# Float64 weights split by bits: from an integer addition on GpSimd to shifts and merges on ScalarE and VectorE, with a scale of 256 left in the weights

## The chip, the core and the metric

The kernel runs on one core of a Trainium2 chip. The metric is the device time of one execution in microseconds. Three runs of the kernel before took 1601.95, 1603.39 and 1604.25 us; their median is 1603.39 us.

The core's engines are named as in the profile: PE (TensorE, the matrix unit; PEld is its weight load), DVE (VectorE), ACT (ScalarE), POOL (GpSimd) and SP (SyncE), which here issues all transfers.

## The reference

q, k and v have 8 batches of 8 heads of 576 tokens of 64 numbers, p has 32 packed queries for each batch and head, all in float32. With a softmax over the last axis, the reference computes

```python
p_packed = sm_attn(p, k, v)
x = sm_attn(q, p_packed, p_packed)
h = x @ w_in1
x = (h / (1 + exp(-h))) @ w_out1
h = x @ w_in2
out = (h * cos(h)) @ w_out2
```

x is laid out as 4608 tokens by 512. Both MLPs go from 512 to 2048 and back to 512. The four weight matrices come as float64, a type in which no engine of the kernel computes, so each weight has to be put together from its two 32-bit words. The low word is the first of the two. The high word holds the sign, 11 bits of exponent and the top 20 bits of the mantissa.

## The kernel before, in words

**Stages.** Tokens are worked on in blocks of 384 in the first MLP (three blocks for each pair of batches, four pairs) and of 512 in the second (nine blocks). Each block goes through the 16 chunks of 128 of the hidden size. So the first MLP has 192 steps (function first, line 850) and the second 144 (function second, line 925). Each step computes h for one chunk in PSUM, applies the activation, splits the result into a rounded part and a rest (split, line 518), and adds its product with w_out to the four accumulators acc. Each product is made of three matmuls (mm3, line 502), on the rounded part and the rest of both operands. For the first MLP w_in1 is multiplied by the packed values of each batch ahead of time (products, line 811), so that a step needs only the second softmax's result a and this product.

**The start.** Nothing of the first MLP can run before the first batch's attention and the first weights are done. At the start the first pair's 48 steps are cut into four groups of 12, one for each quarter of the hidden size. Each group needs four units of w_in1 (w1_unit, line 559) and four of w_out1 (wout1_unit, line 564). Meanwhile the second batch of the first pair goes through its attention. The weights of the second MLP are converted during the last pair (w2_unit, line 567), stored to memory as float32 pairs (w2dram), and loaded again when the second MLP begins.

**The conversion** is decode, lines 533 to 548. A unit is 128 partitions by 512 weights. There are 16 units of w_in1, 16 of w_out1 and 32 of the second MLP. For each unit, SP loads the words into a ring of tiles (wd; at the start also six tiles wde). Then

- ScalarE copies the absolute value of the high word, read as float32, to y (line 540);
- VectorE limits y to the range of the exponents that float32 can hold (a tensor_scalar, max and min), then shifts it left by 3 and masks it (a second tensor_scalar, on integers);
- ScalarE or VectorE, as the planner chooses, turns the low word into its top three bits, as an integer (lines 543 to 545);
- VectorE merges sign and top exponent bit of the high word with these three bits (a scalar_tensor_tensor on integers);
- GpSimd adds the two integers (line 547).

y is a tile named w or w1e for w_in1 and wy for the others. For wy, decode_parts (line 550) then copies the rounded part on ScalarE or VectorE and subtracts it on VectorE. w_in1's y goes to the matmuls of products and, through SP, to memory (w1dram).

**The order.** All instructions are first recorded in a Plan (line 79). Each has an engine, a price in ns (price, line 153) and the instructions that it must wait for. Some have two possible engines: a copy may go to ScalarE or VectorE, and the subtraction of split and two more element-wise steps may go to VectorE or GpSimd (combine, line 513). Due times of PE's steps follow from the list DUE (line 421) by interpolation, and those of all other instructions are worked back from them (order, line 358). A simulated run (schedule, line 277) then takes, on each free engine, the ready instruction that is due first; eight rounds are tried and the best is taken. The result is one fixed order for each engine's queue, SP's among them. In this simulated run, a VectorE instruction whose operands all lie in SBUF is charged extra when it begins while GpSimd is busy (lines 333 to 335).

All instructions are issued from one helper line, so every row of the trace has L194, and rows are told apart by their tiles.

Of the kernel before, what the change touches and what calls it, by code (L numbers as in the profile page):

```python
# [12 lines left out]
F32 = mybir.dt.float32  # L13
F32R = mybir.dt.float32r
I32 = mybir.dt.int32
U32 = mybir.dt.uint32
# [10 lines left out]

REBIAS = 896 << 20  # L30
WORD_MIN, WORD_MAX = (float(x) for x in np.array([REBIAS, REBIAS + 0x0FEFFFFF], np.int32).view(np.float32))


def f32(ap):
# [44 lines left out]
class Plan:  # L79
# [197 lines left out]
    def schedule(self, rank, reverse=False):  # L277


        ops = self.ops  # L280
        n = len(ops)
        if reverse:
            before, after = [o.after for o in ops], [o.before for o in ops]
        else:
            before, after = [o.before for o in ops], [o.after for o in ops]
        left = [len(a) for a in after]
        ready, start, taken = [0.0 if reverse else o.release for o in ops], [0.0] * n, [False] * n
        free = {e: 0.0 for e in (self.PE, self.DVE, self.ACT, self.POOL, self.DMA, self.NONE)}
        queue = {e: [] for e in free}
        coming = [(ready[i], i) for i in range(n) if not left[i]]  # L290
        heapq.heapify(coming)
        t = wire = 0.0
        done = 0

        def head(e):

            q = queue[e]
            while q and taken[q[0][1]]:
                heapq.heappop(q)
            return q[0][1] if q else None  # L300

        def take(e):

            q, aside = queue[e], []
            while (i := head(e)) is not None:
                heapq.heappop(q)
                o = ops[i]
                if reverse or not o.choice:
                    break
                end = t + o.choice[e][0] + (FAVOUR if e == self.DVE else -FAVOUR)  # L310
                if not any(f != e and head(f) == i and max(free[f], t) + o.choice[f][0] < end for f in o.choice):
                    break
                aside.append((rank[i], i))
            for x in aside:
                heapq.heappush(q, x)
            return i

        while done < n:
            while coming and coming[0][0] <= t:
                i = heapq.heappop(coming)[1]  # L320
                for e in (ops[i].engine,) if reverse else ops[i].choice or (ops[i].engine,):
                    heapq.heappush(queue[e], (rank[i], i))
            idle = True
            for e in queue:
                i = take(e) if free[e] <= t else None
                if i is None:
                    continue
                o = ops[i]
                if o.choice and not reverse:
                    o.engine, o.cost, o.emit = e, o.choice[e][0], [o.choice[e][1]]  # L330
                taken[i], start[i] = True, t
                end = t + o.cost
                if e == self.DVE and o.sbuf and not reverse and free[self.POOL] > t:
                    both = min(free[self.POOL] - t, o.cost / self.SHARED)
                    end += both * (1 - self.SHARED)
                free[e] = end
                if e == self.DMA:
                    if reverse:
                        wire = max(t, wire) + o.issue
                        end = wire + self.WIRE + o.cost  # L340
                    else:
                        end = wire = max(end + self.WIRE, wire) + o.issue
                        free[e] = max(free[e], wire - AHEAD)
                if reverse:
                    start[i] = end
                for j in before[i]:
                    lat = self.latency(ops[j], o) if reverse else self.latency(o, ops[j])
                    ready[j] = max(ready[j], end + lat)
                    left[j] -= 1
                    if not left[j]:  # L350
                        heapq.heappush(coming, (ready[j], j))
                done += 1
                idle = False
            if idle:
                t = min([free[e] for e in queue if free[e] > t and head(e) is not None] + [c[0] for c in coming[:1]])
        return start
# [30 lines left out]
def attention_mlps_kernel(  # L387
# [30 lines left out]
    SCALE = 1.0 / math.sqrt(D)  # L418
    plan = Plan(nc)

    DUE = [40e3, 205e3, 378e3, 550e3, 718e3]

    LATER = 380e3
    V, A, T, G, DMA = plan.V, plan.A, plan.T, plan.G, plan.D
# [108 lines left out]
    def decode(src, y):  # L533

        wd = rings["wd"]()
        flat = wd.rearrange("p f t -> p (f t)")
        DMA.dma_start(flat.rearrange("p (c f) -> p c f", c=src.shape[1]) if len(src.shape) == 3 else flat, src)
        lo, hi = wd[:, :, 0], wd[:, :, 1]
        y, yf = y.bitcast(I32), y.bitcast(F32)
        A.activation(yf, hi.bitcast(F32), AF.Abs)  # L540
        V.tensor_scalar(yf, yf, WORD_MIN, WORD_MAX, op0=ALU.max, op1=ALU.min)
        V.tensor_scalar(y, y, 3, 0x3FFFFFF8, op0=ALU.logical_shift_left, op1=ALU.bitwise_and)
        with plan.either():
            A.activation(lo, lo.bitcast(U32), AF.Copy, scale=2.0**-29)
            V.tensor_scalar(lo, lo.bitcast(U32), 2.0**-29, None, op0=ALU.mult)
        V.scalar_tensor_tensor(lo, hi, -(1 << 30), lo, op0=ALU.bitwise_and, op1=ALU.bitwise_or)
        G.tensor_tensor(y, y, lo, ALU.add)
        return flat

    def decode_parts(src, dst=None):  # L550
# [299 lines left out]
    def first(s):  # L850
# [15 lines left out]
        plan.due = None  # L866

        t = gfs()
        A.activation(t, h, AF.Tanh, scale=0.5)
        V.scalar_tensor_tensor(t, t, 1.0, h, op0=ALU.add, op1=ALU.mult)  # L870
        g = gs()
        split(g, t)
# [5 lines left out]
        if end:  # L878
            t0 = (pr * NA + blk) * TA
            dst = ypart[part - 1] if part else ydram  # L880
            for dm in range(KC):
                t = ysbs()
                with plan.either():
                    A.activation(t, acc[dm][:, :TA], AF.Copy, scale=0.5)
                    V.tensor_scalar(t, acc[dm][:, :TA], 0.5, None, op0=ALU.mult)
                DMA.dma_start(dst[dm, :, t0 : t0 + TA], t)


# [36 lines left out]
    def second(s):  # L925
# [8 lines left out]
            mm3(h, (w[:, 0, c], w[:, 1, c]), (y[:, 0], y[:, 1]), kc == 0, kc == KC - 1)  # L934
        plan.due = None
        n = nring()
        A.activation(n, h, AF.Copy, scale=INV_2PI, bias=ROUND)
        V.tensor_scalar(n, n, ROUND, None, op0=ALU.subtract)
        r = rring()
        V.scalar_tensor_tensor(r, n, -TWO_PI_HI, h, op0=ALU.mult, op1=ALU.add)  # L940
        V.scalar_tensor_tensor(r, n, -TWO_PI_LO, r, op0=ALU.mult, op1=ALU.add)
        V.tensor_scalar(r, r, 4.0, -4.0, op0=ALU.min, op1=ALU.max)
        A.activation(r, r, AF.Abs)
        A.activation(r, r, AF.Sin, scale=-1.0, bias=half_pi)
        V.tensor_tensor(r, r, h, ALU.mult)
        g = g2ring()
        split(g, r)
# [1 line left out]
        for t in range(4):  # L949
# [4 lines left out]
            if fc == FC - 1:  # L954
                o = oring()
                if t % 2:
                    V.tensor_copy(o, acc[t])
                else:
                    A.copy(o, acc[t])
                r0 = order[i] * TB + t * P  # L960
                DMA.dma_start(out[r0 : r0 + P, :], o)

# [152 lines left out]
```

## Time and profile before

| | us |
|---|---|
| median of three runs | 1603.39 |
| the profiled execution | 1603.95 |
| its span, first to last instruction | 1602.1 |
| PE busy | 1565.0 (98%) |
| VectorE busy | 1108.7 (69%) |
| ScalarE busy | 755.6 (47%) |
| GpSimd busy | 267.4 (17%) |

The span is the time from the first to the last instruction of the profiled execution; what the execution's time has beyond it lies before and after. An engine is busy while an instruction of its runs; busy shares over the whole span are averages of stages with different limits, so the rows below are mostly for one stage. A VectorE instruction that is held up by another engine counts as busy all the while. The mean duration of a group is that of one instruction from its start to its end; consecutive instructions overlap by some tens of ns.

### The profile page before, as it was taken

To read this page: it belongs to the slowest core of one execution; us is meant where nothing else is said; L and a number is where in the kernel's file an instruction comes from. 1 tells how busy PE (TensorE), PEld (TensorE's weight loads), DVE (VectorE), ACT (ScalarE), POOL (GpSimd) and SP (SyncE) were. 2 spreads that over 40 slices of the span, in tenths; PEclk is the share of its full clock that TensorE was granted. 3 is DMA by queue.
4 is the path that set the end of the run, shared out by engine and by line. 5 is a ranking of instruction groups with operands and counts; after the bars stand their busy time and mean duration, and the time that the engine had idled before them with its cause. 6 is when DMAs were issued, how large, how long until landed. Compare 5 with 4: busy or idle time off the path is not lost.

```text
span 1602.1 us, 24478 instructions
## 1 busy us (share of the span) xinstructions
PE 1565.0 (98%) x9320; PEld 1348.7 (84%) x9320; DVE 1108.7 (69%) x1957; ACT 755.6 (47%) x1388; POOL 267.4 (17%) x216
## 2 busy tenths in 40 slices
PE   9878999999999999999999999999999999999999
PEld 7567888899888998789988888888888888888887
DVE  5998667553689678884456767676776777676766
ACT  5764554433455555544344544444444544444443
POOL 1544101000133223321001000010010111130100
PEclk9978999999999999999999999999999999999999
DMA  9665366210675567645730101000010303010000
GB/s 253 219 194 159 102 129 152 80 43 23 126 215 180 172 185 157 212 171 164 255 127 0 54 0 49 5 21 33 19 54 8 105 21 94 18 57 4 17 10 27
DMA packets 213622, 156.80 MB, mean 98 GB/s; under 512 B 153600, under 2 KB 178688, under 8 KB 213504
## 3 DMA queue, kind: packets, MB, share of 16 engines
q1 hardware_dynamic: 213504, 155.23, 33.3%
q8 instruction: 73, 1.20, 0.3%
q14 instruction: 45, 0.37, 0.1%
HBM read 108.27 MB, written 46.92 MB: 97 GB/s over the span
## 4 chain that ended last, share of the span: by engine, by line
PE 88%; DVE 8%; issue 1%; ACT 1%; DMA 1%; POOL 1%; SPq 0%; DVEq 0%; POOLq 0%; ACTq 0%
PE acc L194 47%; PE hb L194 24%; PE sb L194 9%; PE mb L194 9%; DVE w L194 1%; DVE wy L194 1%; DVE wde L194 1%; DVE wd L194 1%; DVE g L194 1%; DVE big L194 1%; DVE r L194 1%; DVE gf L194 0%; DVE rsb L194 0%; ACT r L194 0%; SPq L194 0%
## 5 line engine op out<-in xcount | busy, mean ns | idle before, releaser
L194 PE MATMUL acc<-g,w 128*128 128x384 f32 x2304 | 461.5, 342 | 4.3 <-ACT ysb L194 2.4
L194 PE MATMUL acc<-w,g 128*128 128x512 f32 x1728 | 464.4, 389 | 0.1
L194 PEld LDWEIGHTS acc<-g,w 128*128 128x128 f32 x2304 | 400.1, 190 | 36.9 <-issue 20.9
L194 PEld LDWEIGHTS acc<-w,g 128*128 128x128 f32 x1728 | 323.8, 188 | 68.7 <-ACT o L194 0.8
L194 PE MATMUL hb<-a,w 128*128 128x384 f32 (+1 forms) x1536 | 271.2, 311 | 21.7 <-ACT a L194 11.1
L194 PEld LDWEIGHTS hb<-a,w 128*128 128x128 f32 x1536 | 237.0, 194 | 35.5 <-ACT a L194 13.6
L194 ACT ACTIVATE r<-r 128x512 f32<-128x512 f32 x144 | 91.0, 632 | 322.4 <-DVE r L194 322.4
L194 PE MATMUL hb<-y,w 128*128 128x512 f32 x864 | 239.4, 389 | 0.0
L194 PEld LDWEIGHTS hb<-y,w 128*128 128x128 f32 x864 | 162.2, 188 | 33.7
L194 ACT CAST g<-gf 128x384 fp32r<-128x384 f32 x171 | 87.7, 513 | 176.9 <-PE acc L194 150.7
L194 POOL TENSOR_TENSOR g<-r,g 128x512 fp32r<-128x512 f32 x51 | 66.4, 1301 | 567.4 <-ACT g L194 512.9
L194 DVE TENSOR_TENSOR g<-gf,g 128x384 fp32r<-128x384 f32 x142 | 85.5, 602 | 99.6 <-ACT g L194 98.0
L194 DVE SCALAR_TENSOR_TENSOR gf<-gf,hb 128x384 f32<-128x384 f32 x192 | 105.0, 548 | 63.6 <-ACT gf L194 62.1
L194 ACT ACTIVATE gf<-hb 128x384 f32<-128x384 f32 x192 | 94.0, 490 | 91.9 <-PE hb L194 90.8
L194 DVE SCALAR_TENSOR_TENSOR r<-n,r 128x512 f32<-128x512 f32 x144 | 124.1, 862 | 3.0
L194 PE MATMUL sb<-y,w 128*128 128x512 f32 x432 | 121.4, 389 | 0.0
L194 PE MATMUL mb<-y,w 128*128 128x512 f32 x432 | 121.0, 389 | 0.0
L194 POOL TENSOR_TENSOR g<-gf,g 128x384 fp32r<-128x384 f32 x50 | 59.7, 1194 | 352.0 <-ACT g L194 288.7
L194 ACT ACTIVATE r<-r,half_pi 128x512 f32<-128x512 f32 x144 | 104.2, 723 | 4.4
L194 DVE TENSOR_TENSOR r<-r,hb 128x512 f32<-128x512 f32 x72 | 49.4, 686 | 81.9 <-ACT r L194 81.7
L194 PEld LDWEIGHTS sb<-y,w 128*128 128x128 f32 x432 | 81.1, 188 | 16.7
L194 PEld LDWEIGHTS mb<-y,w 128*128 128x128 f32 x432 | 81.0, 188 | 16.6
(190 smaller groups left out, 1645.8 us busy)
## 6 DMA issues: line engine op xcount, KB each, us to landing
w2dram<-wd SPq DMA_DIRECT2D x32, 512.0 KB, 2.9
w<-w2dram SPq DMA_DIRECT2D x32, 512.0 KB, 4.2
wd<-in_moe_w_in SPq DMA_DIRECT2D x24, 512.0 KB, 4.5
w<-w1dram SPq DMA_DIRECT2D x48, 256.0 KB, 3.7
wd<-in_moe_w_out SPq DMA_DIRECT2D x20, 512.0 KB, 4.0
ydram<-ysb SPq DMA_DIRECT2D x48, 192.0 KB, 2.2
yst<-ydram SPq DMA_DIRECT2D x36, 256.0 KB, 2.7
out<-o SPq DMA_DIRECT2D x36, 256.0 KB, 2.1
```

Of the source, the lines that this page charges most:

```text
L194: run = lambda: emit(*[real(x) for x in args], **{k: real(x) for k, x in kw.items()})
```

## The change

ScalarE now scales while it takes the absolute value (by 2^-111), which moves the exponent to where a shift by 3 leaves it right, except for a factor 256 that stays in all four weights. VectorE limits y from above only. The low word always goes to ScalarE, with a changed scale and a bias. VectorE then merges the sign with the low bits, and in one more scalar_tensor_tensor shifts y by 3 and merges it with that. GpSimd has no part in it. The 256 is taken out later by constants: in the Tanh and in the scale of ysb in the first MLP, in the range reduction, the Sin and the copies of o in the second. Two edits concern the planner: the extra charge for VectorE beside GpSimd, and the five numbers of DUE.

```diff
-REBIAS = 896 << 20
-WORD_MIN, WORD_MAX = (float(x) for x in np.array([REBIAS, REBIAS + 0x0FEFFFFF], np.int32).view(np.float32))
+DOWN = 2.0**-111
+WORD_MAX = float(np.array([0x0FEFFFFF], np.int32).view(np.float32)[0])
+WEIGHT = 256.0
...
                 if e == self.DVE and o.sbuf and not reverse and free[self.POOL] > t:
-                    both = min(free[self.POOL] - t, o.cost / self.SHARED)
-                    end += both * (1 - self.SHARED)
+                    end += (free[self.POOL] - t) * self.SHARED
...
-    DUE = [40e3, 205e3, 378e3, 550e3, 718e3]
+    DUE = [38e3, 203e3, 376e3, 548e3, 716e3]
...
-        A.activation(yf, hi.bitcast(F32), AF.Abs)
-        V.tensor_scalar(yf, yf, WORD_MIN, WORD_MAX, op0=ALU.max, op1=ALU.min)
-        V.tensor_scalar(y, y, 3, 0x3FFFFFF8, op0=ALU.logical_shift_left, op1=ALU.bitwise_and)
-        with plan.either():
-            A.activation(lo, lo.bitcast(U32), AF.Copy, scale=2.0**-29)
-            V.tensor_scalar(lo, lo.bitcast(U32), 2.0**-29, None, op0=ALU.mult)
-        V.scalar_tensor_tensor(lo, hi, -(1 << 30), lo, op0=ALU.bitwise_and, op1=ALU.bitwise_or)
-        G.tensor_tensor(y, y, lo, ALU.add)
+        A.activation(yf, hi.bitcast(F32), AF.Abs, scale=DOWN)
+
+        A.activation(lo, lo.bitcast(U32), AF.Copy, scale=2.0**-29 * 0.8749, bias=0.5)
+        V.tensor_scalar(yf, yf, WORD_MAX, None, op0=ALU.min)
+        V.scalar_tensor_tensor(lo, hi, -(1 << 31), lo, op0=ALU.bitwise_and, op1=ALU.bitwise_or)
+        V.scalar_tensor_tensor(y, y, 3, lo, op0=ALU.logical_shift_left, op1=ALU.bitwise_or)
...
-        A.activation(t, h, AF.Tanh, scale=0.5)
+        A.activation(t, h, AF.Tanh, scale=0.5 / WEIGHT)
...
-                    A.activation(t, acc[dm][:, :TA], AF.Copy, scale=0.5)
-                    V.tensor_scalar(t, acc[dm][:, :TA], 0.5, None, op0=ALU.mult)
+                    A.activation(t, acc[dm][:, :TA], AF.Copy, scale=0.5 / WEIGHT**2)
+                    V.tensor_scalar(t, acc[dm][:, :TA], 0.5 / WEIGHT**2, None, op0=ALU.mult)
...
-        A.activation(n, h, AF.Copy, scale=INV_2PI, bias=ROUND)
+        A.activation(n, h, AF.Copy, scale=INV_2PI / WEIGHT, bias=ROUND)
...
-        V.scalar_tensor_tensor(r, n, -TWO_PI_HI, h, op0=ALU.mult, op1=ALU.add)
-        V.scalar_tensor_tensor(r, n, -TWO_PI_LO, r, op0=ALU.mult, op1=ALU.add)
-        V.tensor_scalar(r, r, 4.0, -4.0, op0=ALU.min, op1=ALU.max)
+        V.scalar_tensor_tensor(r, n, -TWO_PI_HI * WEIGHT, h, op0=ALU.mult, op1=ALU.add)
+        V.scalar_tensor_tensor(r, n, -TWO_PI_LO * WEIGHT, r, op0=ALU.mult, op1=ALU.add)
+        V.tensor_scalar(r, r, 4.0 * WEIGHT, -4.0 * WEIGHT, op0=ALU.min, op1=ALU.max)
...
-        A.activation(r, r, AF.Sin, scale=-1.0, bias=half_pi)
+        A.activation(r, r, AF.Sin, scale=-1.0 / WEIGHT, bias=half_pi)
...
-                    V.tensor_copy(o, acc[t])
+                    V.tensor_scalar(o, acc[t], WEIGHT**-2, None, op0=ALU.mult)
-                    A.copy(o, acc[t])
+                    A.activation(o, acc[t], AF.Copy, scale=WEIGHT**-2)
```

## Rows read from the trace of the kernel before

**Rows 1.** Stretch, length; busy PE, PEld, DVE, ACT, POOL; clock, DMA share, GB/s

```profile
0.00:40.00 40.00, 36.93 (x508) 30.52 (x508) 22.76 (x64) 20.14 (x44) 6.20 (x10) 1.00 0.98 253
40.00:140.00 100.00, 74.31 (x587) 60.16 (x587) 95.90 (x155) 63.42 (x125) 52.37 (x35) 0.86 0.62 189
140.00:450.00 310.00, 310.00 (x2318) 278.63 (x2317) 183.98 (x357) 139.15 (x299) 25.50 (x22) 0.99 0.43 105
450.00:735.00 285.00, 280.24 (x1977) 252.47 (x1977) 224.09 (x411) 147.56 (x293) 85.63 (x70) 0.99 0.60 183
735.00:1500.00 765.00, 764.95 (x3505) 645.74 (x3504) 514.77 (x862) 342.44 (x563) 89.94 (x74) 1.00 0.17 54
1500.00:1602.10 102.10, 98.55 (x435) 81.17 (x433) 67.16 (x113) 42.87 (x68) 7.74 (x6) 0.99 0.06 21
```

**Rows 2.** Waits of PE, whole span: us in total, times, longest us

```profile
PE hb L194 <- ACT a L194: 11.1, 5, 4.7
```

**Rows 3.** Groups on VectorE, 40 to 140 us: busy us, mean ns, idle before

```profile
L194 DVE SCALAR_TENSOR_TENSOR wde<-wde 128x512 int32<-128x512 int32 x18 | 17.9, 994 | 0.0
L194 DVE TENSOR_TENSOR w<-wy,w 128x512 fp32r<-128x512 f32 x12 | 10.3, 862 | 0.0
L194 DVE TENSOR_SCALAR wy<-wy 128x512 f32<-128x512 f32 x12 | 7.3, 612 | 0.0
L194 DVE TENSOR_SCALAR wy<-wy 128x512 int32<-128x512 int32 x12 | 7.2, 601 | 0.0
L194 DVE TENSOR_SCALAR w<-w 128x512 int32<-128x512 int32 x8 | 6.3, 792 | 0.0
L194 DVE TENSOR_SCALAR w<-w 128x512 f32<-128x512 f32 x8 | 4.5, 572 | 0.0
L194 DVE TENSOR_SCALAR w1e<-w1e 128x512 f32<-128x512 f32 x4 | 4.2, 1080 | 0.0
L194 DVE CAST w<-wy 128x512 fp32r<-128x512 f32 x2 | 3.1, 1556 | 1.7 <-POOL wy L194 1.7
L194 DVE TENSOR_SCALAR wd<-wd 128x512 int32<-128x512 uint32 x1 | 1.5, 1544 | 0.0
L194 DVE TENSOR_SCALAR wde<-wde 128x512 int32<-128x512 uint32 x3 | 1.3, 420 | 0.0
```

**Rows 4.** Tile wd, whole span: ns min/median/max, first, last start

```profile
L194 DVE SCALAR_TENSOR_TENSOR wd<-wd x44: 623/686/1327, 13.1 to 730.1; 128x512 int32<-128x512 int32 x44
L194 DVE TENSOR_TENSOR wd<-wy,wd x32: 673/684/1514, 454.8 to 733.4; 128x512 fp32r<-128x512 f32 x32
```

**Rows 5.** Timeline of GpSimd and VectorE: start us, duration us

```profile
57.30 2.03 POOL L194 TENSOR_TENSOR wy<-wy,wde 128x512 int32<-128x512 int32 x1 [0.36 <-DVE wy L194]
58.08 1.54 DVE L194 TENSOR_SCALAR wd<-wd 128x512 int32<-128x512 uint32 x1
```

**Rows 6.** GpSimd busy on wy, on w, on w1e, 40 to 140 us

```profile
40.00:140.00 100.00, 17.89 (x12) 0.86 0.62 189
40.00:140.00 100.00, 11.97 (x8) 0.86 0.62 189
40.00:140.00 100.00, 5.83 (x4) 0.86 0.62 189
```

**Rows 7.** A group on ScalarE, 40 to 140 us

```profile
L194 ACT ACTIVATE wde<-wde 128x512 int32<-128x512 uint32 x15 | 10.2, 694 | 0.0
```

**Rows 8.** Chain of waits, two pieces: start us, us, what

```profile
93.67 1.69 POOL w1e L194
...
104.59 0.56 DVE g L194
...
110.59 1.42 POOL w1e L194
...
120.41 1.49 DVE w L194
```

**Rows 9.** SP queue waits, 0 to 160 us: us, times, longest

```profile
SPq L194 <- POOL wy L194: 20.6, 8, 5.3
```

## The prediction

> **What bounds the kernel now.** I read the busy time by stage first [rows 1]. Six stretches tell the whole story. Between 140 and 450 us, and again between 735 and 1500 us, PE is busy for 310.00 of 310 and 764.95 of 765 us: there nothing that another engine saves can shorten the run, and nothing that it gains is lost again either. PE is idle for 3.07 us in the first 40 us, for 25.69 us between 40 and 140 us, for 4.76 us between 450 and 735 us, and for 3.55 us at the end. Of its 37.1 us of idle time, 25.7 us lie in the one stretch of 100 us in which the weights of the first MLP are converted. In that stretch VectorE is busy for 95.90 us of 100, ScalarE for 63.42, GpSimd for 52.37, and the DMA engines carry 0.62 of their time. So VectorE is the bound of this stretch, and PE is the bound after it. The waits have a second price there: PE's granted clock averages 0.86 in this stretch, after 1.00 in the 40 us before it [rows 1], so that PE runs a part of it at the lower of its two levels. PE's longest waits in all are for the tile a, 11.1 us in five waits [rows 2]; a is a batch's attention result, which VectorE makes in between the conversions.
>
> Then I looked at what VectorE's 95.9 us consist of [rows 3]. The conversion's instructions cost far more than their clean size. A tensor_scalar over 128x512 takes 0.42 us where nothing disturbs it (three first conversions of the low word), but the same instruction on wd took 1.54 us, and the groups on w and w1e have means of 0.57 to 1.08 us. The bitwise scalar_tensor_tensor on wde has a mean of 0.99 us, where the median over the whole run is 0.686 us for the same shape on wd [rows 4]. With 0.686 us for it, 0.684 us for the subtraction [rows 4] and 0.42 us for the tensor_scalars (and, as an estimate, for the casts of the same size), the excess of the ten groups of [rows 3], in their order, is 5.55 + 2.09 + 2.26 + 2.16 + 2.94 + 1.14 + 2.52 + 2.26 + 1.08 + 0.00 = 22.0 us. One pair of rows shows where it comes from [rows 5]: GpSimd starts an addition into wy at 57.30 us that ends at 59.33; VectorE starts a tensor_scalar at 58.08, in the middle of it, and ends it at 59.62, some 0.3 us after GpSimd is done. VectorE stood still while GpSimd worked.
>
> **The change, part by part.**
>
> The addition on GpSimd goes. In the bound stretch it stands there 12 + 8 + 4 = 24 times with 17.89 + 11.97 + 5.83 = 35.69 us [rows 6], of GpSimd's 52.37 us [rows 1]. The 22.0 us that VectorE loses are 0.42 us for each us that GpSimd works, so these additions cost VectorE 35.69 x 0.42 = 15.0 us. This is where the trace has no direct price, so I bound it: below by nothing (the planner could give the free GpSimd as many optional subtractions as it loses), above by the whole 35.69 us, if every us of GpSimd stopped VectorE. I take 15.0 us, the share the rows show, since much of what VectorE runs there (transposes, reductions, reads of PSUM) shows no excess.
>
> Beside that share stands a rule. The Trainium skill, SBUF — State Buffer, section Who interferes with whom, says that the port pair shared by VectorE and GpSimd is an exclusive lock: whoever starts first keeps it for the whole instruction, and the other waits in full. The pair [rows 5] agrees with it; by it alone the term would go to its upper end, 35.69 us, and the sum below to some 25 us.
>
> Two tensor_scalars and one scalar_tensor_tensor on VectorE become one tensor_scalar (min alone) and two scalar_tensor_tensors (sign and low bits, then shift and or). No row shows shift and or together with two inputs; the nearest is the scalar_tensor_tensor with and/or on the same type and size, 0.623 at least, 0.686 in the median, 1.327 at most [rows 4]. I take 0.686 and keep the other two for the range. For 24 conversions this adds 24 x (0.686 - 0.42) = 6.4 us to VectorE. Its bounds are 24 x 0.20 = 4.9 and 24 x 0.91 = 21.8 us.
>
> The low word always goes to ScalarE. In the stretch four of the 24 ran on VectorE (the last two groups of [rows 3]), so VectorE sheds 4 x 0.42 = 1.7 us. ScalarE takes four more, which its 36.6 idle us [rows 1] hide. If that cover were gone, they would cost four instructions of a size that takes ScalarE 0.69 us [rows 7]. The added scale and bias change no shape; I take nothing for them, between a gain of nothing and a loss that the same idle time hides.
>
> VectorE's balance in the stretch: 15.0 - 6.4 + 1.7 = 10.3 us less, 85.6 of 100 us. It stays the busiest engine: ScalarE comes to 66, PE to 74, and the DMA engines, which carried 0.98 of their time in the first 40 us [rows 1], would need 62 / 0.98 = 63 us for the same bytes.
>
> Not all of it is on the path. The chain of waits leaves VectorE twice: from 93.67 to 104.59 us (an addition on GpSimd, a row of issues on SP, a load of k) and from 110.59 to 120.41 us (GpSimd) [rows 8], 20.7 us together. I count the rest, 79%: 10.3 x 0.79 = 8.1 us. What the second of these pieces, itself made of GpSimd's work, might give I leave to the range.
>
> SP's queue issues in order and waited for the additions, 20.6 us for those into wy alone up to 160 us [rows 9]; what stands behind is the next loads and the stores of y. With the addition gone it waits for the last scalar_tensor_tensor on VectorE. I count nothing for it, because loads are not what PE waits for.
>
> The second MLP's weights, 32 conversions between 450 and 735 us, go the same way. VectorE has 60.9 idle us there, which hide the 32 x 0.266 = 8.5 us that are added at most. PE can gain its 4.76 idle us and no more; between that and nothing I take 1 us, because these waits may as well end with the next batch's attention.
>
> The weights kept at scale 256 change constants only (Tanh, Sin, the range reduction, ysb). The 36 copies of o become multiplications of the same 128x512 from the same PSUM banks on the same two engines. I take nothing: PE is busy throughout from 735 to 1500 us, and only the last ones lie in the 3.55 us at the end.
>
> The planner. All five due times move by the same 2 us, and every other due time is derived from these, so the ranks stay as they are; I cost it at nothing. The new charge for a VectorE instruction beside GpSimd is no longer limited by the instruction's own cost. It and the new instructions give a new order everywhere. No row prices an order. One badly placed instruction costs what PE's worst wait for a cost, 4.7 us [rows 2]; I take zero and keep 4.7 us on both sides for the range.
>
> The sum: 8.1 + 1 = 9.1 us. The profiled execution took 1603.95 us (span 1602.1), so it would take 1594.9; it lies 0.56 us above the median of the three runs, 1603.39, and against that the forecast is 1594. A difference under 0.2%, 3.2 us, can hardly be told from no change here.
>
> **The rivals.**
>
> The full lock, chance 0.18. If GpSimd's whole time comes back, VectorE loses 35.69 - 4.7 = 31.0 us, 24.5 on the path, with the w2 stretch 25.5: 1578. The pair of [rows 5] speaks for it, the ten groups with only 22.0 us for 52.37 us against.
>
> The path is taken over, chance 0.13. VectorE gets faster and then waits: for loads, as in the 20.7 us of [rows 8], or within the serial chain of the attention for whose result PE waited 11.1 us. Then the 8.1 us turn into idle time on VectorE, and 0 to 3 us remain: 1602. Against it stands that VectorE had hardly any idle time in the stretch, so that its queue, not its inputs, held those results back.
>
> VectorE pays and is not relieved, chance 0.09. The planner lets GpSimd take a subtraction of split whenever it is free, and now it is free. If it takes 35.7 us of these, VectorE stands still as long as before, and the conversion's own growth is left: 4.7 us in the stretch, 3.7 on the path, 1607. It decides once the relief is under 4.7 of 35.69 us, or 0.13 us per us of GpSimd. Against it: each subtraction moved takes its own time off VectorE, and the stretch has few of them.
>
> That the change doesn't do what it says can only concern the due times, as above.
>
> **How the numbers follow.** The forecast has 0.60. Its own range is 1588 to 1599: the order's 4.7 us either way, and below (6.4 - 4.9) x 0.79 = 1.2 us more from the scalar_tensor_tensor's lower end. Its upper end, (21.8 - 6.4) x 0.79 = 12.2 us, would need every one to be held up like the worst; that is the last rival's case. Reaching down to the full lock gives 1578; reaching up past the taken-over path to a small loss, 1604. Left out are the lossy case and the tails, under 2 in 10. Faster by over 0.2%: the forecast but for its upper edge, and the lock, 0.58 + 0.18 + a little of the taken-over path, 0.79. Slower: the last rival, partly, and a bad order, 0.09. Same: 0.12.
>
> **What would show it.** Right: GpSimd's busy time between 40 and 140 us falls to a third or half, the tensor_scalars of the conversion come near 0.42 us, the new scalar_tensor_tensor is near 0.69 us, SP no longer waits for GpSimd's additions, PE's idle time falls from 37 to about 28 us, mostly before 140 us, and its granted clock there rises from 0.86. Wrong: VectorE is still busy for over 92 of those 100 us with means near 1 us (not relieved), or it has over 10 us of idle time there while PE waits as long as now (path taken over), or PE idles again after 140 us in a place where it did not (the order).

## The result and the profile after

Four runs of the changed kernel took 1582.27 to 1583.66 us, median 1582.84; the kernel before, on the same chip, 1602.67. The ratio is 0.9877, with a 95% interval of 0.9860 to 0.9894: 19.8 us faster, twice the 9.1 us of the sum. The profiled execution has a span of 1580.5 us, 21.6 less than before.

The stages of the changed kernel up to 735 us, in the columns of [rows 1]:

```profile
0.00:40.00 40.00, 36.91 (x508) 30.80 (x508) 22.64 (x63) 21.30 (x45) 0.70 (x6) 1.00 0.97 259
40.00:140.00 100.00, 87.11 (x695) 74.89 (x696) 94.64 (x173) 73.72 (x146) 23.66 (x15) 0.91 0.72 221
140.00:450.00 310.00, 310.00 (x2327) 276.41 (x2326) 186.89 (x363) 138.51 (x294) 19.29 (x17) 1.00 0.43 105
450.00:735.00 285.00, 282.94 (x2013) 257.66 (x2012) 216.47 (x393) 151.05 (x302) 40.77 (x34) 1.00 0.60 182
```

Between 40 and 140 us PE runs 695 matmuls instead of 587 and is idle for 12.89 us instead of 25.69. Its clock there is 0.91 instead of 0.86. GpSimd's work falls to 45%. VectorE is as busy as before, 94.64 us, but it finishes 173 instructions instead of 155. The page gives PE 1558.0 busy us for the same 9320 matmuls, where it had 1565.0. So the 21.6 us are 14.6 us less idle time of PE (37.1 to 22.5) and 7.0 us less busy time. That the busy time is the clock is read from the first MLP's two main groups of matmuls, whose number and shape are the same in both kernels, while their means are shorter in the changed one (columns as in [rows 3]; the kernel before, then the changed kernel):

```profile
L194 PE MATMUL acc<-g,w 128*128 128x384 f32 x2304 | 461.5, 342 | 4.3 <-ACT ysb L194 2.4 <-POOL g L194 0.9 <-DVE g L194 0.5
L194 PE MATMUL hb<-a,w 128*128 128x384 f32 x768 | 167.4, 342 | 8.6 <-DVE gf L194 5.9 <-ACT a L194 1.5 <-POOL a L194 1.0
```

```profile
L196 PE MATMUL acc<-g,w 128*128 128x384 f32 x2304 | 455.8, 339 | 0.6 <-ACT g L196 0.5
L196 PE MATMUL hb<-a,w 128*128 128x384 f32 x768 | 165.5, 339 | 4.5 <-ACT a L196 2.1 <-DVE gf L196 0.9 <-POOL a L196 0.9
```

Where the time is won can be read from the copies of finished accumulators into ysb, four for each block of the first MLP (in the first pair for each quarter of a block). The three rows below are for the tile ysb in the kernel before, up to 157, 285 and 830 us; then the same up to 140, 267 and 803 us in the changed kernel. The columns are count, ns, first and last start.

```profile
L194 ACT ACTIVATE ysb<-acc x16: 479/486/512, 81.3 to 154.5; 128x384 f32<-128x384 f32 x16
L194 ACT ACTIVATE ysb<-acc x48: 470/490/512, 81.3 to 283.8; 128x384 f32<-128x384 f32 x48
L194 ACT ACTIVATE ysb<-acc x82: 469/490/516, 81.3 to 823.3; 128x384 f32<-128x384 f32 x82
```

```profile
L196 ACT ACTIVATE ysb<-acc x16: 473/492/500, 77.7 to 137.4; 128x384 f32<-128x384 f32 x16
L196 ACT ACTIVATE ysb<-acc x47: 473/491/511, 77.7 to 266.1; 128x384 f32<-128x384 f32 x47
L196 ACT ACTIVATE ysb<-acc x83: 468/491/514, 77.7 to 800.8; 128x384 f32<-128x384 f32 x83
```

(The copies missing from 48 and 84 ran on VectorE.) The changed kernel is 17.1 us ahead at the 16th copy, 17.7 us at the end of the first pair, and 22.5 us at the end of the first MLP. So 17.7 us come from the start. The other 4.8 us lie behind it, where the second MLP's weights are converted. The second MLP itself gives nothing.

The 4.8 us hold less firmly than the 17.7. Two more traces have the same queues as the two kernels (the kernel before with the planner's edits alone, and the changed kernel without them, both below). Their copies at the end of the first pair and of the first MLP:

```profile
L194 ACT ACTIVATE ysb<-acc x48: 470/488/499, 81.5 to 284.0; 128x384 f32<-128x384 f32 x48
L194 ACT ACTIVATE ysb<-acc x82: 470/491/513, 81.5 to 820.8; 128x384 f32<-128x384 f32 x82
```

```profile
L196 ACT ACTIVATE ysb<-acc x47: 477/492/509, 77.7 to 266.1; 128x384 f32<-128x384 f32 x47
L196 ACT ACTIVATE ysb<-acc x83: 472/492/512, 77.7 to 801.0; 128x384 f32<-128x384 f32 x83
```

Here the start gives 17.9 us, and what lies between it and the end of the first MLP only 1.9 us. The execution of the kernel before that [rows 1] shows had a clock of 0.97 from 500 to 550 us, where the other execution of these queues had 1.00.

The conversion's groups on VectorE between 40 and 140 us, in the changed kernel, beside [rows 3]:

```profile
L196 DVE SCALAR_TENSOR_TENSOR wde<-wde 128x512 int32<-128x512 int32 x18 | 12.4, 698 | 0.0
L196 DVE SCALAR_TENSOR_TENSOR wy<-wy,wde 128x512 int32<-128x512 int32 x12 | 9.8, 820 | 0.1
L196 DVE TENSOR_TENSOR w<-wy,w 128x512 fp32r<-128x512 f32 x12 | 8.9, 744 | 0.0
L196 DVE TENSOR_SCALAR wy<-wy 128x512 f32<-128x512 f32 x14 | 8.6, 614 | 0.2 <-ACT wy L196 0.2
L196 DVE TENSOR_SCALAR w<-w 128x512 f32<-128x512 f32 x8 | 3.8, 504 | 0.0
L196 DVE SCALAR_TENSOR_TENSOR w<-w,wd 128x512 int32<-128x512 int32 x4 | 3.4, 884 | 0.0
```

The merge of sign and low bits on wde, 0.994 us in the mean before, is at 0.698. The excess of these six groups over the sizes of the prediction is 0.05 + 1.57 + 0.69 + 2.72 + 0.44 + 0.66 = 6.1 us; the conversion's seven smaller groups add less than 1 us. Before, ten groups had 22.0. What is left stands beside the 23.66 us of optional steps that GpSimd still takes there. The new step, in its largest group on the tile wy over the whole span (ns min/median/max), has in the median the price that was taken for it:

```profile
L196 DVE SCALAR_TENSOR_TENSOR wy<-wy,wd x36: 623/688/1503, 133.1 to 703.7; 128x512 int32<-128x512 int32 x36
```

SP's queue, from 0 to 160 us, now waits for VectorE's last step where it waited for GpSimd's addition [rows 9]:

```profile
SPq L196 <- DVE wy L196: 23.4, 7, 4.8
```

### The profile page after: what moved, and what is told of

Same layout as the page of the kernel before. It is cut to its first block, busy times and chain, and to the rows that moved or that the text cites. A ratio compares the mean times of both kernels' runs of the same rounds, so it can differ in the third digit from the quotient of the medians.

```text
span 1580.5 us, 24329 instructions
## 1 busy us (share of the span) xinstructions
PE 1558.0 (99%) x9320; PEld 1344.4 (85%) x9320; DVE 1093.7 (69%) x1946; ACT 762.3 (48%) x1403; POOL 177.8 (11%) x148
## 4 chain that ended last, share of the span: by engine, by line
PE 77%; DVE 11%; ACT 3%; issue 1%; DMA 1%; POOL 0%; SPq 0%; DVEq 0%; ACTq 0%; POOLq 0%
PE acc L196 42%; PE hb L196 21%; PE sb L196 8%; PE mb L196 7%; DVE r L196 4%; ACT r L196 2%; DVE g L196 1%; DVE wy L196 1%; DVE w L196 1%; DVE wd L196 1%; DVE n L196 1%; DVE gf L196 0%; DVE wde L196 0%; DVE big L196 0%; DMA wd<-in_moe_w_in 0%
## 5 line engine op out<-in xcount | busy, mean ns | idle before, releaser
L196 PE MATMUL acc<-g,w 128*128 128x384 f32 x2304 | 455.8, 339 | 0.6 <-ACT g L196 0.5
L196 POOL TENSOR_TENSOR g<-r,g 128x512 fp32r<-128x512 f32 x45 | 58.6, 1303 | 565.2 <-ACT g L196 509.0
L196 POOL TENSOR_TENSOR g<-gf,g 128x384 fp32r<-128x384 f32 x43 | 53.4, 1241 | 494.3 <-ACT g L196 421.6
```

The costliest lines, as they stand in the source:

```text
L196: run = lambda: emit(*[real(x) for x in args], **{k: real(x) for k, x in kw.items()})
```

## The experiments

### The instructions or the order

Two runs separate the new instructions from the new order of the queues. In the first, the plan is made for the old conversion, but the new instructions are issued:

```diff
...
+        def low(d, x):
+            nc.scalar.activation(d, x, AF.Copy, scale=2.0**-29 * 0.8749, bias=0.5)
+        def merge(d, x, z):
+            nc.vector.scalar_tensor_tensor(d, x, 3, z, op0=ALU.logical_shift_left, op1=ALU.bitwise_or)
+        plan.add(plan.DVE, "tensor_scalar", lambda d, x: None, (y, y), {})
+        with plan.either():
+            plan.add(plan.ACT, "activation", low, (lo, lo.bitcast(U32)), {})
+            plan.add(plan.DVE, "tensor_scalar", low, (lo, lo.bitcast(U32)), {})
...
+        plan.add(plan.POOL, "tensor_tensor", merge, (y, y, lo), {})
```

> The order of all queues is the one of the kernel before; the instructions of the conversion are the changed ones (the scalar_tensor_tensor stands on VectorE where the order had GpSimd's addition, the second tensor_scalar is left out, the low word goes to ScalarE in its old place). Theory A, the instructions do it (no addition on GpSimd that stops VectorE): 1582 to 1588 us, PE idle before 140 us falls from 28.8 to about 16 us. Theory B, the planner's new order does it: 1598 to 1603 us.

It took 1591.57 us, ratio 0.9925 (0.9910 to 0.9940) to the kernel before. Neither theory had it: the instructions alone give 12 us, and the new order the rest, some 8 to 9 us. The run's stage from 40 to 140 us, and its copies up to 146, 275 and 815 us:

```profile
40.00:140.00 100.00, 83.36 (x640) 70.65 (x639) 86.96 (x162) 68.63 (x135) 19.86 (x13) 0.86 0.68 200
```

```profile
L196 ACT ACTIVATE ysb<-acc x16: 482/492/506, 79.7 to 143.8; 128x384 f32<-128x384 f32 x16
L196 ACT ACTIVATE ysb<-acc x48: 470/492/506, 79.7 to 272.9; 128x384 f32<-128x384 f32 x48
L196 ACT ACTIVATE ysb<-acc x82: 470/492/513, 79.7 to 811.1; 128x384 f32<-128x384 f32 x82
```

VectorE is relieved by 8.9 us and then stands idle for 13 us of the stretch, where it had 4.1 us before. Its longest waits there are 3.4 us for a load of p and 2.5 us for ScalarE. That this comes from an order made for slower steps is the reading; no run shows it by itself. Even so the run gains 10.7 us at the 16th copy and 12.2 us by the end of the first MLP. The order of the changed kernel fills that idle time again (94.64 us). Its PE is also better fed: the page of this run has 1563.3 us of PE, that of the changed kernel 1558.0, so 5.3 us of what the order gives are shorter matmuls, by the reading above at the higher clock (0.91 against 0.86 in the stretch).

The second run has the new order, but the old last step:

```diff
+        def merge(d, x, n, z):
+            nc.vector.tensor_scalar(d, x, n, None, op0=ALU.logical_shift_left)
+            nc.gpsimd.tensor_tensor(d, d, z, ALU.add)
+        plan.add(plan.DVE, "scalar_tensor_tensor", merge, (y, y, 3, lo), {})
-        V.scalar_tensor_tensor(y, y, 3, lo, op0=ALU.logical_shift_left, op1=ALU.bitwise_or)
```

> The order of the changed kernel, but the last scalar_tensor_tensor of each conversion becomes a shift on VectorE (tensor_scalar) and an addition on GpSimd. Theory A: the gain goes although the order is the new one, 1597 to 1608 us, VectorE's means in the conversion rise to those of before. Theory B: most of the gain stays, 1583 to 1589 us.

It took 1615.9 us, 1.0079 (1.0064 to 1.0094): more than the kernel before. Theory A had the sign, not the size. The addition costs 33 us in this order, though a shift (0.42 us) is less work for VectorE than a merge (0.69 us). At the 16th copy the run stands at 154.6 us, like the kernel before, and at the end of the first MLP at 834.2 us, 10.9 us behind it. So its order is better for the start only with the instructions it was made for, and it is worse than the old order for additions in the last pair.

### The planner's own edits

```diff
-                    both = min(free[self.POOL] - t, o.cost / self.SHARED)
-                    end += both * (1 - self.SHARED)
+                    end += (free[self.POOL] - t) * self.SHARED
-    DUE = [40e3, 205e3, 378e3, 550e3, 718e3]
+    DUE = [38e3, 203e3, 376e3, 548e3, 716e3]
```

These edits alone, in the kernel before:

> The kernel before with the planner's two edits alone (the charge beside GpSimd and the due times). Theory A: a new order of old instructions, 1600 to 1606 us. Theory B: 1588 to 1597 us.

It took 1603.22 us, ratio 0.9999 (0.9990 to 1.0009). The reverse, the changed kernel without them:

> The changed kernel with the planner's two edits undone. Theory A: within 4 us of the changed kernel, 1579 to 1587 us. Theory B: 1590 to 1600 us.

It took 1582.99 us, 0.9875 (0.9858 to 0.9891), the time of the changed kernel. In both pairs the queues are the same, instruction for instruction. The due times move together, as the prediction says. The charge, however, is never made: the condition in add asks whether the memory's name ends in SBUF, and the program calls that memory MemoryType.SB. So the whole new order comes from the changed instructions, those of the conversion.

### What the addition on GpSimd costs, and what VectorE's time is worth

All three runs of this group keep the changed kernel's order. In the first, VectorE does one more merge, which changes nothing, in each of the 32 conversions for the first MLP:

```diff
...
+            if extra:
+                nc.vector.scalar_tensor_tensor(z, z, 0, z, op0=ALU.logical_shift_left, op1=ALU.bitwise_or)
```

> The order of the changed kernel; in each of the 32 conversions for the first MLP VectorE does one more scalar_tensor_tensor of 128x512 (low or low, which changes nothing), 24 of them between 40 and 140 us, about 0.69 us each, 16 us in the stretch. Theory C, VectorE's queue sets the end of this stretch and about 0.8 of its time passes into the whole: 10 to 18 us more than the changed kernel, 1593 to 1601 us. Theory D, VectorE now has slack on the path: under 5 us more, 1583 to 1588 us.

It took 1602.84 us, ratio 0.9993 (0.9984 to 1.0003) where the changed kernel has 0.9877: 18 to 20 us more. The 16th copy starts at 157.4 us, 20.0 us late. All 32 extra merges are 32 x 0.686 = 22.0 us on VectorE, so 0.91 us come through for each us added (0.97 by the 30 that have started before this copy). This is theory C and a little more: the 24 conversions inside the stretch, 16.5 us, are less than the 20.0 us, so those outside it count too.

In the second, GpSimd adds each finished low word to a tile that nobody reads:

```diff
...
+            if extra:
+                nc.gpsimd.tensor_tensor(side, side, z, ALU.add)
```

> The order of the changed kernel; in each of the 32 conversions for the first MLP GpSimd adds the finished low word to a tile that nobody else reads, about 1.35 us each, so that GpSimd works as long as before the change but no result waits for it. Theory A1, GpSimd costs VectorE its time by holding it up (0.42 us for each us of GpSimd, 24 x 1.35 x 0.42 = 14 us in the stretch): 8 to 18 us more than the changed kernel, 1591 to 1601 us. Theory A2, what the addition cost was its place in the chain of each conversion (a longer way to the finished weight): 0 to 4 us more, 1583 to 1587 us. The full lock: 24 x 1.35 = 32 us on VectorE, 1605 us or more.

It took 1607.93 us, 1.0025 (1.0014 to 1.0036): 24 to 25 us more than the changed kernel. That is far from A2, beyond theory A1's range, and inside the range given for the full lock (1605 us or more). So the time alone does not tell the two prices of the hold-up apart; the rows have to. GpSimd's side additions up to 165 us, four of the conversion's groups on VectorE from 40 to 140 us, and the 16th copy:

```profile
L555 POOL TENSOR_TENSOR side<-side,wde 128x512 int32<-128x512 int32 x20 | 30.2, 1509 | 23.4 <-DVE wde L196 16.1 <-issue 6.2 <-POOL side L555 0.7
L555 POOL TENSOR_TENSOR side<-side,wd 128x512 int32<-128x512 int32 x10 | 16.0, 1595 | 17.5 <-DVE wd L196 17.2
```

```profile
L196 DVE SCALAR_TENSOR_TENSOR wde<-wde 128x512 int32<-128x512 int32 x15 | 13.4, 898 | 0.0
L553 DVE SCALAR_TENSOR_TENSOR wy<-wy,wde 128x512 int32<-128x512 int32 x11 | 11.6, 1062 | 0.1
L196 DVE TENSOR_SCALAR wy<-wy 128x512 f32<-128x512 f32 x11 | 9.5, 868 | 0.0
L553 DVE SCALAR_TENSOR_TENSOR w<-w,wd 128x512 int32<-128x512 int32 x3 | 4.7, 1598 | 0.0
```

```profile
L196 ACT ACTIVATE ysb<-acc x16: 476/486/495, 90.7 to 162.7; 128x384 f32<-128x384 f32 x16
```

The conversion's steps on VectorE are back at means of 0.87 to 1.6 us, though nobody needs what GpSimd adds. The 16th copy comes 25.3 us late for 46.2 us of side additions up to then, 0.55 us for each us of GpSimd. The pages of both runs show that this is the hold-up: with the same 1946 instructions VectorE is busy for 1120.1 us here and for 1093.7 us in the changed kernel, 26.4 us more, while GpSimd has 224.0 us instead of 177.8, 46.2 us more. That is 0.57 us for each us, nearer to the prediction's 0.42 than to the full lock's 1; the range for the full lock was met because there are 30 additions up to then, at 1.5 us and more each, not 24 at 1.35 us. (A tile of words is free for the next load only after its side addition; no run separates that, and little of the 25.3 us is left for it.)

In the third, the limiting tensor_scalar (min) is left out of all conversions, and with it the limit for weights beyond float32's range:

```diff
-        V.tensor_scalar(yf, yf, WORD_MAX, None, op0=ALU.min)
+        plan.add(plan.DVE, "tensor_scalar", lambda d, x: None, (yf, yf), {})
```

> The order of the changed kernel, with the limiting tensor_scalar (min) left out of all conversions; this leaves out the limit for weights beyond float32's range. VectorE has 24 x 0.42 = 10 us less to do between 40 and 140 us. Theory C: 5 to 9 us less than the changed kernel, 1574 to 1578 us. Theory D: 0 to 3 us less, 1580 to 1583 us.

It took 1577.17 us, 0.9829 (0.9813 to 0.9845), 6 to 8 us less than the changed kernel, inside theory C's range. But only 4.1 us of it are there at the 16th copy (133.3 us) for 32 x 0.42 = 13.4 us less on VectorE, or 0.31 us for each us; the rest comes behind the first pair, where the second MLP's conversions lack the step too. So in the start VectorE's time costs 0.91 when added and gives back 0.31 when taken away: in the changed kernel VectorE is no longer the only bound of the start. The stretch now has it busy for 86.9 us, 7.7 us less.

### The second MLP's weights

The old last step, in the new order, only in the 32 conversions of the last pair:

```diff
...
+            if add:
+                nc.vector.tensor_scalar(d, x, n, None, op0=ALU.logical_shift_left)
+                nc.gpsimd.tensor_tensor(d, d, z, ALU.add)
```

> The order of the changed kernel, with shift on VectorE and addition on GpSimd only in the 32 conversions of the second MLP's weights. From the ends of the blocks in the run with the addition everywhere, half of its loss lies there: 1594 to 1602 us. If this stretch has slack, as the forecast had it (PE idle 2 to 5 us there): 1583 to 1586 us.

It took 1599.31 us, 0.9974 (0.9961 to 0.9986), some 16 us more than the changed kernel: the first range. Its stage from 450 to 735 us:

```profile
450.00:735.00 285.00, 271.74 (x1899) 244.24 (x1898) 206.99 (x381) 142.81 (x288) 79.15 (x64) 0.99 0.58 174
```

PE is idle for 13.26 us here, where it was idle for 2.06 us in the changed kernel and for 4.76 us before. VectorE has more idle time than in either, 78 us. So the cover that the prediction counted on here, VectorE's idle time, does not hide a later result in this order. In the kernel before, with its additions in the old order, PE was idle for only 4.76 us here.

### What in the plan makes the new order better

Three runs issue the changed kernel's instructions and change only what the plan believes. First, the low word may again go to VectorE:

```diff
+        with plan.either():
             A.activation(lo, lo.bitcast(U32), AF.Copy, scale=2.0**-29 * 0.8749, bias=0.5)
+            V.tensor_scalar(lo, lo.bitcast(U32), 2.0**-29 * 0.8749, 0.5, op0=ALU.mult, op1=ALU.add)
```

> The changed kernel, planned anew, but the planner may again give the low word to VectorE. Theory E, the new order's 8 us come from moving the low word off VectorE: 1586 to 1592 us, with a good part of the low words on VectorE. Theories F and G, they come from elsewhere: within 3 us of the changed kernel, 1580 to 1586 us.

1583.61 us, 0.9873 (0.9858 to 0.9888). The plan gave VectorE only 7 of the 64 low words, so theory E was hardly put to the test, but the free choice would not have mattered. Second, each unit is ready later in the plan:

```diff
+        plan.record(plan.NONE, lambda: None, [plan.region(y)], [plan.region(y)], 1224, 0)
...
```

> The changed kernel with its own instructions, but the plan is made as if each converted unit were ready 1224 ns later (a step on no engine, as long as the plan's price of the old addition). Theory F, the new order is better because the plan knows that a unit is ready earlier: 1587 to 1593 us, like the old order with the new instructions. Theory G, because the plan has GpSimd free: within 3 us of the changed kernel, 1580 to 1586 us.

1586.44 us, 0.9890 (0.9876 to 0.9905): by the medians 3.6 us slower, short of theory F's range; the intervals of the two ratios overlap, and by the ratios the difference is 2 us. Third, GpSimd is busy in the plan:

```diff
+        plan.record(plan.POOL, lambda: None, [("side", (0, 128, 1))], [plan.region(lo)], 1224, 0)
...
```

> The changed kernel with its own instructions, but the plan is made as if GpSimd were busy for 1224 ns after each conversion with something that no result waits for. Theory G, the plan needs GpSimd free for the subtractions: 1587 to 1593 us. Theory F: within 3 us of the changed kernel, 1580 to 1586 us.

1583.09 us, 0.9870 (0.9855 to 0.9885): no effect, theory G falls. What remained was whether the run with the old order merely had its last merge too late in VectorE's queue. There the merge was now issued as soon as both its inputs were:

```diff
...
+        def shift(d, x, z):
+            done.append(1)
+            if len(done) == 2:
+                merge(d, x, z)
...
```

> As the run with the old order and the new instructions, but the last scalar_tensor_tensor stands on VectorE as soon as both its inputs are made there, not where the old order had GpSimd's addition. Theory H, what that run lacked against the changed kernel beyond the 3.6 us of the late plan was the late place of this step in VectorE's queue: 1584 to 1588 us. Theory I, the old order is worse in many other places: 1589 to 1593 us, as without it.

1590.83 us, 0.9911 (0.9896 to 0.9926), as without it, so theory H falls. That leaves theory I, many other places, but where they are no run shows. A later finish in the plan may explain 2 to 4 us of the order's 8 to 9; the rest is not traced to one of the plan's beliefs, and the order of SP's loads, which the plan makes too, was not tested by itself.

### The planner's charge, made to work

```diff
-        self.ops[-1].sbuf = all(str(raw(x).space).endswith("SBUF") for x in outs + ins)
+        self.ops[-1].sbuf = all(str(raw(x).space).endswith("SB") for x in outs + ins)
```

In the changed kernel:

> The changed kernel, with the planner's charge for VectorE beside GpSimd made to work (it compares the memory's name with SBUF, while the program calls it SB, so that no instruction is ever charged; the queues are the same with the charge at 0 and at 1). Theory A1, holding up is what costs: the plan that counts it gains some of the 9.5 us that VectorE still loses between 40 and 140 us, 1574 to 1581 us. If the plan's other errors weigh as much: 1581 to 1590 us.

1579.6 us (1574.95 to 1582.32), 0.9838 (0.9816 to 0.9860). By its median this is the fastest version that computes everything, but two of its four runs, the profiled one among them, took 1582 us like the changed kernel, and the intervals touch. So a gain is not shown. With the whole of GpSimd's remaining time as the charge (SHARED = 1.0):

> The changed kernel with the working charge for VectorE beside GpSimd, at the whole of GpSimd's remaining time instead of half. If the held-up time is nearly the whole of GpSimd's, as the run with the side additions says (25 us for 32 additions): 1573 to 1579 us, a little under the half charge. If the charge overstates it: 1580 to 1586 us.

1585.67 us, 0.9879 (0.9863 to 0.9896): no better than without a charge. And the kernel before, its conversion untouched, with its own charge made to work:

> The kernel before, unchanged in its conversion, with its own charge made to work. If the plan's blindness to the hold-up cost the kernel before much of what the change won: 1588 to 1598 us. If not, since the additions have to run somewhere beside VectorE: 1599 to 1606 us.

1588.63 us, 0.9900 (0.9886 to 0.9915). That is 15 us, three quarters of what the change won, with every addition still on GpSimd. Its stage from 40 to 140 us shows how, in the columns of [rows 1]:

```profile
40.00:140.00 100.00, 81.57 (x650) 68.08 (x649) 97.14 (x153) 67.07 (x135) 47.28 (x35) 0.90 0.67 203
```

GpSimd works nearly as long as before (47.28 us against 52.37) and VectorE is just as full, but PE has 81.57 us instead of 74.31. The hold-up itself has not gone. The ten groups of [rows 3] exceed the prediction's sizes by 22.5 us here, 22.0 before; three of them:

```profile
L194 DVE SCALAR_TENSOR_TENSOR wde<-wde 128x512 int32<-128x512 int32 x18 | 14.3, 792 | 0.0
L194 DVE TENSOR_SCALAR wy<-wy 128x512 f32<-128x512 f32 x12 | 12.1, 1010 | 0.0
L194 DVE TENSOR_SCALAR w<-w 128x512 int32<-128x512 int32 x8 | 6.6, 856 | 0.0
```

What has changed is the plan: what VectorE does first, and what it leaves to others (GpSimd has 334.0 us over the whole run instead of 267.4). PE gets its operands earlier. The copies up to 148 and 810 us are 9.2 us ahead of the kernel before at the 16th and 14.7 us at the end of the first MLP:

```profile
L194 ACT ACTIVATE ysb<-acc x16: 472/491/504, 76.8 to 145.3; 128x384 f32<-128x384 f32 x16
L194 ACT ACTIVATE ysb<-acc x83: 465/491/512, 76.8 to 808.6; 128x384 f32<-128x384 f32 x83
```

So VectorE's lost time came with the additions, but what it cost the program was in large part an order made by a plan that did not count it. The change's 20 us are therefore no measure of what the addition must cost.

## Why the prediction was right and wrong

The sign, the place and the mechanism were right: the start is where PE waits, VectorE is what it waits for, and GpSimd's additions are what swells VectorE's steps. The size was not. 1582.84 us lies below the forecast's own range, 1588 to 1599 us, and inside only the wide one, which reaches down to 1578 us for the full lock. The gain is 19.8 us where the sum had 9.1.

**The step that failed is the planner's.** The prediction said that no row prices an order, and took zero with 4.7 us on both sides, the price of one badly placed instruction. In the old order, the one the sum was made for, the new instructions gave 12 us; the new order gave 8 to 9 us more, 6.4 us of them by the 16th copy (143.8 to 137.4). Why this order is so much better stays open. The prediction also gave the new charge a share in that order; it has none.

**The start was sized too low, 8.1 us for 10.9.** The run in the old order is 10.9 us ahead at the end of the first pair (283.8 to 272.9). VectorE's balance in the stretch was about right there: 86.96 us busy, 85.6 forecast. What it was taken to be worth was small. The sum counted the 24 conversions between 40 and 140 us, while the run with extra merges shows that those outside count too. And it passed on 79% of VectorE's time, by the pieces of the chain that lie elsewhere [rows 8], where that run shows 0.91 for time added. The price of GpSimd's time, 0.42, was of the right size: the side additions show 0.55 to 0.57.

**PE's clock was named and then not priced.** "The waits have a second price", says the prediction, and no term of the sum has it. It was 7.0 us of the 21.6. This is no third part beside the two above: 5.3 of the 7.0 us came with the new order (1563.3 to 1558.0).

**The last pair** was given 1 us. Against the execution of [rows 1] it is 1.3 us in the old order (12.2 less 10.9) and 4.8 us in the new one (22.5 less 17.7). PE's idle time between 450 and 735 us, which the prediction took as the bound, fell by 2.7 us (4.76 to 2.06). Against the other execution of the old queues the new order has 1.9 us, and the new instructions in the old order lose 1.4 us (820.8 to 811.1, less 284.0 to 272.9). So the term cannot be told from 1 us.

**The signs.** Of the signs of being wrong, one half came true: VectorE is busy for 94.64 of the 100 us, over the 92 of the first. It does not mean what the prediction said it would. The means are 0.50 to 0.88 us, not near 1, and the run in the old order has VectorE at 86.96 us; the new order fills the relief with more work (173 instructions for 155).

**Right as they stood:** the new scalar_tensor_tensor (0.688 us in the median for 0.686), the due times without effect, SP's queue waiting for VectorE as long as it did for GpSimd (23.4 us for 20.6). The second MLP, with its copies of o and its constants for the scale of 256, took 0.9 us longer (22.5 us ahead before it, 21.6 after it), and by the other two traces the same (19.8 and 18.9). Whether ScalarE hides its four more low words was not tested by itself.

**The rivals.** The full lock had the nearest number, 1578, by a way that the runs don't bear out: the new instructions alone gave 12 us, not 25, and 46.2 us of side additions cost 25.3. Its nearness is luck. The path taken over is what the run in the old order shows in part, 13 us of idle VectorE; the new order took that back. The lossy rival needed less relief than 0.13 us for each us of GpSimd, and the side additions show four times that.

## What to carry to other kernels

Where VectorE bounds a stretch, count a good part of GpSimd's time as VectorE's too, here 0.42 to 0.57 us for each us. Where a program plans its own queues, changed instructions are a new plan: its worth is not zero, and the idle time of the engine that bounds the whole run (here PE), with the matmuls that run at the lower clock around it, is what it can win back. And before a planner's term is weighed, see whether any queue changes when it is set to nothing. A lost us is not a fixed price either: with the hold-up as large as before, another plan of the same conversion won 15 us.

## What was not expected of the hardware

The hold-up goes both ways. In the changed kernel an addition of 128x384 on GpSimd takes 1.0 to 1.2 us when left alone, and 3.60 us here (timelines of GpSimd and of VectorE; start, duration):

```profile
119.76 3.60 POOL L196 TENSOR_TENSOR g<-gf,g 128x384 fp32r<-128x384 f32 x1 [9.93 <-ACT g L196]
123.62 1.16 POOL L196 TENSOR_TENSOR g<-gf,g 128x384 fp32r<-128x384 f32 x1 [0.27 <-ACT g L196]
```

```profile
119.38 0.68 DVE L196 SCALAR_TENSOR_TENSOR wy<-wy,wde 128x512 int32<-128x512 int32 x1
119.98 1.28 DVE L196 SCALAR_TENSOR_TENSOR w<-w,wd 128x512 int32<-128x512 int32 x2
121.19 1.28 DVE L196 SCALAR_TENSOR_TENSOR wde<-wde 128x512 int32<-128x512 int32 x2
122.39 0.55 DVE L196 SCALAR_TENSOR_TENSOR gf<-gf,hb 128x384 f32<-128x384 f32 x1
122.86 1.04 DVE L196 SCALAR_TENSOR_TENSOR wde<-wde 128x512 int32<-128x512 int32 x1
```

GpSimd has its operands at 119.76, but VectorE runs one merge with two inputs in SBUF after the other, with no gap: one that was under way, and four that begin after 119.76. Only at 122.39 does it turn to a step whose second input is in PSUM. GpSimd ends 0.97 us after that, about its undisturbed time, and the next merge, begun at 122.86, takes 1.04 us instead of 0.69. An addition that starts at 105.17 and takes 3.25 us shows the same: it ends 0.96 us after such a step of VectorE begins, at 107.46. The Trainium skill, SBUF — State Buffer, section Who interferes with whom, says that a VectorE instruction with two inputs in SBUF contends with a GpSimd instruction that reads SBUF, and that whoever issues first has the shared port pair for the whole instruction while the other is fully blocked. The timelines agree that the two engines block each other. As for who is first they differ, if the profile's starts are taken as they are: GpSimd's addition started before four of the merges and still came after them. Over whole stretches the runs show 0.42 to 0.57 us of VectorE for each us of GpSimd, not 1; GpSimd's own time held up, as here, is part of the us that this counts.
